# Linear attention with a gated projection on one core: the softmax statistics of q spread in two half transfers, a third batch sent down the same route, and a new order of all steps

## The chip, the core and the metric

One core of a Trainium2 chip runs one program. The core has TensorE (PE, matmuls, with its weight loads shown as PEld), VectorE (DVE), ScalarE (ACT), GpSimd (POOL), SyncE (SP, which here issues every DMA) and 16 DMA engines. The metric is the device time of one execution in microseconds (us); lower is better.

## What is computed

There are 8 batches of 8 heads, 576 positions and 64 channels per head, all float32 (the weights arrive as 64-bit words and are turned into float32 on the chip).

```python
q_s = exp(q - max(q, axis=-1));  q_s = q_s / (sum(q_s, axis=-1) + 1e-9)     # over the 64 channels
k_s = exp(k - max(k, axis=2));   k_s = k_s / (sum(k_s, axis=2) + 1e-9)      # over the 576 positions
kv  = einsum('bhsd,bhse->bhde', k_s, v)
x   = einsum('bhsd,bhde->bhse', q_s, kv)      # then 8 heads side by side: 576 x 512 per batch
gate = sigmoid(sum over 5 taps j of conv_w[j] * x shifted by 4 - j positions)
out  = (gate * (x @ w_val)) @ w_out
```

## The kernel before

The program is a list of about 1,100 short steps, `ORDER`, written out in full; each entry names a function, its indices, the engine (`a` = ACT, `v` = DVE, `p` = POOL) and the buffer slots that it takes (`@n`). Every engine works its own steps strictly in the order of that list, SP its DMAs too, and waits on semaphores wherever a step needs the result or the buffer of another. So the order of the list sets the time.

Per batch `b` the work runs as follows. `load_k`, `k_peak`, `k_row`, `k_spread`, `k_sub` and `k_exp` make the exponentials of k (the column maxima go to DRAM as one row, and a DMA, `k_spread`, brings that row back into all 128 partitions as the tile `kmax`). `kv` multiplies k and v on PE, `kv_norm` scales the result. `attend b g` (L506) makes two of the four x tiles, each in a PSUM bank pair of its own. Each x tile is then read by `x_high` and `x_low` (the value split into two parts for matmuls), `first` and four `tap` steps, which build the gate; a tap with `v` is one DVE instruction (L530), a tap with `a` is a product on ACT (L533) and an addition on POOL (L534). `sigmoid`, `value` (L548, 6 matmuls), `gated` (L553), `g_high`, `g_low`, `project` (L575, 3 matmuls) and `store` finish it.

The softmax of q must end with channels on the partitions, because `attend` contracts over them. There are two routes:

- **By rows and a transpose** (batches 0 to 3): `q_max`, `q_sub`, `q_exp`, `q_sum`, `q_over`, `q_mul` normalise q with positions on the partitions; `q_turn` and `tail_turn` transpose it on PE, and `q_turned` and `tail_turned` copy it out of PSUM on ACT.
- **By rows and channels** (batches 4 to 7): q is loaded a second time with channels on the partitions (`load_qc`, 1152 KB). The row copy gives only statistics: `q_log` makes max + ln(sum), `stat_turn` and `stat_turned` transpose them, `q_row` (L449, L451) writes them to DRAM as two rows of 9,216 bytes, one for each half of the partitions, and `q_spread` (L456) brings them back as a tile `qsp` in which the first row fills partitions 0 to 63 and the second row partitions 64 to 127, 1152 KB. Four `qc_sub` steps (L460, on POOL or DVE) subtract that tile from q, and two `qc_exp` (L464, ACT) finish. `qc_sub` reads all 128 partitions of `qsp`, so it needs both rows' halves.

The spread of a batch is one DMA with the access pattern [2, 64, 2304]: the outermost dimension is the two rows, the second repeats a row 64 times with a step of zero, and the last is the row.

Of the kernel before, what the change touches and what calls it, by code (L numbers as in the profile page):

```python
# [16 lines left out]
B, H, S, D = 8, 8, 576, 64  # L17
# [25 lines left out]
    tail_turned 0 a @5, kv 0 @2, part 3 a @9, load_words 0 @4, field 0 @1, q_mul 0 2 a, part 0 a @0, joined 2,
    w_high 2 a, scaled 0 a, load_kc 1 2 3 @6, q_mul 0 1 p, q_sub 1 4 v, q_mul 0 3 p, q_turn 0 0 @0, load_kc 1 3 4,
    k_top 1 2 @1, k_raise 1 2, q_turned 0 0 a, kv_norm 0 v @0, attend 0 0 @1 @2, k_top 1 3, joined 3, load_kc 1 1 2,
    k_top 1 1, load_words 5 @5, k_raise 1 3, signed 0, field 5 @5, w_low 2 p, warm 0 @1, k_raise 1 1, load_kc 1 0 1,
    k_top 1 0, x_high 0 1 a @6, x_low 0 1, joined 8, first 0 1 a @7, tap 0 1 1 v, tap 0 1 3 v, q_sub 1 3 p,
    tap 0 1 0 v, x_high 0 0 a @0, x_low 0 0, first 0 0 a @4, load_q 5 @7, joined 0, q_turn 0 1 @0, q_turned 0 1 a,
    tap 0 0 1 v, joined 4, tap 0 1 2 a @2, w_high 0 a, q_sub 1 0 p, tap 0 0 2 v, k_raise 1 0, tap 0 0 3 v, w_high 3 a,
    attend 0 1 @0 @2, w_low 3 p, x_high 0 2 a @1, tap 0 0 0 v, warm 11 @0, first 0 2 a @3, tap 0 2 1 v, tap 0 2 3 v,  # L50
    w_high 4 p, w_low 4 p, tap 0 2 0 v, load_words 6 @2, x_low 0 2, tap 0 2 2 a @1, k_tail_turn 1 @1, scaled 5 a,
    warm 6 @0, x_high 0 3 a @3, load_words 7 @4, x_low 0 3, k_turn 1 0 @1, k_turned 1 0 a @1, q_exp 1, part 5 a @6,
# [5 lines left out]
    kv_norm 1 v @1, q_mul 1 3 p, q_mul 1 2 p, q_turn 1 0 @2, scaled 7 a, q_turned 1 0 a, q_turn 1 1 @0,
    q_turned 1 1 a, g_low 0 1 p, load_q 3 @5, load_km 2 0 @7, k_peak 2 0, signed 7, signed 6, load_q 2 @6,
    g_high 0 0 a, load_km 2 1 @4, attend 1 0 @1 @2, load_km 2 3 @8, w_high 5 p, first 1 1 a @1, tap 1 1 0 v,  # L60
    tap 1 1 3 v, w_low 5 p, value 0 2 3 @0, sigmoid 0 2, g_low 0 0 p, value 0 2 0, tap 1 1 2 v, part 7 a @7,
    x_high 1 0 a @5, project 0 0 1 @1, value 0 2 2, x_high 1 1 a @4, x_low 1 1, joined 7, first 1 0 a @6, tap 1 0 0 v,
    part 6 a @5, joined 6, load_v 2 @0, tap 1 1 1 a @0, sigmoid 0 3, k_peak 2 3, tap 1 0 3 v, tap 1 0 2 a @2,
    value 0 2 1, gated 0 2 @8, w_high 6 a, project 0 1 1 @0, w_low 6 p, project 0 0 0, k_peak 2 1, k_row 2, x_low 1 0,
    value 0 3 3 @2, w_high 7 a, value 0 3 1, g_high 0 2 a, g_low 0 2 p, value 0 3 2, q_max 2 @0, tap 1 0 1 a @0,
    value 0 3 0, gated 0 3 @3, attend 1 1 @0 @1, load_k 2 @1, x_high 1 2 a @2, first 1 3 a @4, w_low 7 p, tap 1 3 3 v,
    x_low 1 2, sigmoid 1 1, project 0 1 0, x_high 1 3 a @3, x_low 1 3, g_high 0 3 a, tap 1 3 2 v, load_km 4 0 @2,
    project 0 0 2, first 1 2 a @5, k_spread 2 @8, tap 1 2 2 v, load_km 3 3 @9, project 0 1 2, value 1 2 1 @2,
    k_peak 4 0 @1, value 1 2 0, g_low 0 3 p, value 1 2 2, sigmoid 1 0, tap 1 2 3 v, project 0 0 3, q_sub 2 3 p,
    load_km 3 2 @0, value 1 2 3, store 0 0 a @7, q_sub 2 0 p, project 0 1 3, store 0 1 a @3, project 0 2 0 @1,  # L70
    q_sub 2 2 p, tap 1 2 1 v, tap 1 2 0 v, q_sub 2 4 p, sigmoid 1 2, tap 1 3 0 v, tap 1 3 1 v, project 0 2 1,
    project 0 2 2, project 0 2 3, value 1 3 2 @0, gated 1 2 @2, sigmoid 1 3, k_sub 2 0 v, q_max 3 @1, load_km 4 1 @7,
# [15 lines left out]
    project 0 5 0, load_k 4 @0, q_mul 3 0 p, x_high 2 2 a @3, tap 2 1 1 a @6, tap 2 3 3 v, tap 2 2 0 v, project 0 4 2,
    value 2 2 1 @2, q_mul 3 2 p, q_mul 3 1 a, tap 2 2 1 v, k_spread 4 @0, q_sub 4 1 p, k_exp 3, project 0 4 0,
    q_mul 3 4 p, value 2 2 3, value 2 2 0, k_sub 4 2 p, project 0 4 3, store 0 5 a @4, k_sub 4 0 p, kv 3 @0,  # L90
    q_mul 3 3 a, tap 2 2 2 v, x_low 2 2, value 2 2 2, k_peak 5 1 @0, kv_norm 3 v @1, q_turn 3 0 @1, q_sub 4 4 p,
    sigmoid 2 2, tail_turn 3 @1, tail_turned 3 a @3, q_sub 4 3 p, k_peak 5 3, q_sub 4 2 p, gated 2 2 @6, q_max 5 @1,
# [555 lines left out]
```

## Time and profile before

| what | value |
|---|---|
| median of 3 runs | 403.88 us (403.73 to 403.95) |
| the profiled execution, its own time | 404.08 us |
| its span in the trace | 402.3 us |
| mean granted TensorE clock | 0.868 of full speed |
| DMA traffic | 60.74 MB, 151 GB/s over the span |

The trace is of one execution; start times count from the start of its span. A duration of an instruction is what its engine shows; "idle before" names the event that ended a wait. A row of stretches gives, for each engine, busy time and number of instructions, then the granted TensorE clock as a share of full speed, the mean share of the 16 DMA engines that was busy, and what they moved.

### The profile page before, as it was taken

Reading aid. Unit: us, or ns where it says so; the run is one execution under the profiler, and the core shown is the slowest. Engines: PE = TensorE matmul, PEld = TensorE weight load, DVE = VectorE, ACT = ScalarE, POOL = GpSimd, SP = SyncE. Lnnn points to the kernel's source line nnn. Section 1 sums busy time; section 2 is a strip of 40 time slices with the busy share of each in tenths; the row PEclk is TensorE's granted clock in tenths of the full one; section 3 lists DMA queues with packets and bytes.
Section 4 is the critical chain, followed back from the end, with each engine's and each line's share of the span. In section 5 each row is a group of like instructions: output and inputs, shape, how many; then the busy total and the mean of one; then the engine's idle time right before and its main releaser. Section 6 shows DMA issues by size and latency. Waiting matters only on the chain.

```text
span 402.3 us, 5954 instructions
## 1 busy us (share of the span) xinstructions
PE 299.6 (74%) x2292; PEld 252.9 (63%) x2292; DVE 248.4 (62%) x331; ACT 212.8 (53%) x318; POOL 204.6 (51%) x182
## 2 busy tenths in 40 slices
PE   6565699998969979407950886913977349999998
PEld 6553498787748859306740675912875346989987
DVE  4997698989798877408970377705886034364111
ACT  2885697758779586506720658702725014753110
POOL 3743764898789766008503946006472161856230
PEclk9585889999999998956995696975989959999999
DMA  8997057478765574511621771214601110011022
GB/s 299 416 364 265 28 203 268 101 269 314 171 246 201 149 226 163 173 53 53 204 91 51 261 286 63 100 54 170 222 31 48 76 47 26 28 52 54 26 97 88
DMA packets 17604, 60.74 MB, mean 151 GB/s; under 512 B 2856, under 2 KB 3112, under 8 KB 13864
## 3 DMA queue, kind: packets, MB, share of 16 engines
q1 hardware_dynamic: 17576, 60.36, 42.8%
q8 instruction: 18, 0.29, 0.3%
q14 instruction: 10, 0.08, 0.1%
HBM read 50.83 MB, written 9.52 MB: 150 GB/s over the span
## 4 chain that ended last, share of the span: by engine, by line
DMA 27%; PE 26%; DVE 25%; issue 11%; ACT 7%; POOL 4%; SPq 1%; ACTq 0%; DVEq 0%; POOLq 0%
DMA qsp<-qrow 13%; PE out L575 10%; PE val L548 9%; DVE gate L530 8%; DMA km<-in_k_strided 6%; DMA out<-o 5%; DVE qs L389 3%; DVE kpk L303 2%; DVE g L553 2%; PE x L506 2%; DVE xx L516 2%; PE kv L478 2%; DMA q<-in_q 2%; DVE qm L371 2%; ACT xx L218 1%
## 5 line engine op out<-in xcount | busy, mean ns | idle before, releaser
L530 DVE SCALAR_TENSOR_TENSOR gate<-x,cw,gate 128x575 f32<-128x575 f32 (+3 forms) x94 | 75.2, 810 | 31.7 <-ACT gate L522 25.1
L548 PE MATMUL val<-xx,w_val_hi 128*128 128x288 f32 x512 | 92.4, 304 | 0.0
L548 PEld LDWEIGHTS val<-xx,w_val_hi 128*128 128x128 f32 x512 | 79.1, 198 | 0.0
L548 PE MATMUL val<-xx,w_val_lo 128*128 128x288 f32 x256 | 59.0, 313 | 24.5 <-DVE kvd L490 17.5
L534 POOL TENSOR_TENSOR gate<-gate,far 128x574 f32<-128x574 f32 (+3 forms) x34 | 43.9, 1291 | 45.9 <-ACT far L533 45.5
L548 PEld LDWEIGHTS val<-xx,w_val_lo 128*128 128x128 f32 x256 | 45.6, 199 | 32.8 <-issue 17.7
L575 PE MATMUL out<-w_out_lo,gh 128*128 128x512 f32 x144 | 60.3, 419 | 3.3 <-ACT o L218 3.0
L575 PE MATMUL out<-w_out_hi,gl 128*128 128x512 f32 x144 | 58.3, 405 | 0.0
L575 PE MATMUL out<-w_out_hi,gh 128*128 128x512 f32 x144 | 58.2, 404 | 0.0
L506 PE MATMUL x<-qT,kvd 64*64 64x288 f32 x256 | 25.0, 486 | 40.2 <-ACT far L533 16.8
L460 POOL TENSOR_TENSOR qT<-qT,qsp 128x576 f32<-128x576 f32 x10 | 16.1, 1613 | 71.9 <-DMA qsp<-qrow 71.9
L566 POOL TENSOR_TENSOR gl<-g,gh 128x576 fp32r<-128x576 f32 x27 | 38.2, 1421 | 26.4 <-ACT gh L218 18.2
L506 PEld LDWEIGHTS x<-qT,kvd 64*64 64x64 f32 x256 | 10.5, 152 | 49.6 <-POOL gl L566 16.4
L533 ACT ACTIVATE far<-x,cw 128x574 f32<-128x574 f32 (+3 forms) x34 | 24.7, 740 | 24.1 <-DVE gate L530 14.4
L320 POOL TENSOR_TENSOR k<-k,kmax 128x512 f32<-128x512 f32 (+1 forms) x32 | 36.3, 1150 | 0.8 <-DMA kmax<-krow 0.2
L575 PEld LDWEIGHTS out<-w_out_lo,gh 128*128 128x128 f32 x144 | 27.9, 194 | 12.6 <-issue 6.6
L553 DVE TENSOR_TENSOR g<-val,gate 128x576 f32<-128x576 f32 x32 | 24.0, 751 | 17.7 <-ACT gate L537 9.3
L478 PE MATMUL kv<-v,k 128*64 128x65 f32 x512 | 21.2, 244 | 15.6 <-DVE g L553 11.3
L575 PEld LDWEIGHTS out<-w_out_hi,gl 128*128 128x128 f32 x144 | 28.0, 194 | 7.5 <-POOL gl L566 1.1
L460 DVE TENSOR_TENSOR qT<-qT,qsp 128x576 f32<-128x576 f32 x6 | 4.5, 754 | 45.2 <-DMA qsp<-qrow 45.2
L379 POOL TENSOR_TENSOR q<-q,qm 128x512 f32<-128x512 f32 (+1 forms) x32 | 30.8, 979 | 2.3 <-issue 2.2
L522 ACT ACTIVATE gate<-x,cw 128x576 f32<-128x576 f32 x27 | 20.0, 747 | 20.6 <-DVE xx L220 6.8
(81 smaller groups left out, 503.2 us busy)
## 6 DMA issues: line engine op xcount, KB each, us to landing
v<-in_v SPq DMA_DIRECT2D x8, 1170.0 KB
out<-o SPq DMA_DIRECT2D x36, 256.0 KB
q<-in_q SPq DMA_DIRECT2D x7, 1152.0 KB
km<-in_k_strided SPq DMA_DIRECT2D x24, 288.0 KB
k<-in_k SPq DMA_DIRECT2D x6, 1152.0 KB
qT<-in_q_channels SPq DMA_DIRECT2D x4, 1152.0 KB
qsp<-qrow SPq DMA_DIRECT2D x4, 1152.0 KB
kc<-in_k_channels SPq DMA_DIRECT2D x8, 288.0 KB
```

The lines of the kernel that those rows point to most:

```text
L320: engine(e).tensor_sub(kk[r, a], kk[r, a], top[r, m])
L379: engine(e).tensor_sub(qq, qq, spread(T["qm", b], h0, h1))
L460: engine(e).tensor_sub(t, t, T["qsp", b][:, n * S:n * S + S])
L478: nc.tensor.matmul(acc[h * D:(h + 1) * D, u, i], kk[:, g], vv[:, g], start=(c == 0), stop=False)
L506: nc.tensor.matmul(x[half][o, t0:t1], kvd[b % 2][r, n], T["qT", b][r, n, t0:t1], start=True, stop=True)
L530: nc.vector.scalar_tensor_tensor(out=a, in0=x, scalar=w, in1=a, op0=ALU.mult, op1=ALU.add)
L533: nc.scalar.activation(far, x, AF.Copy, scale=w)
L534: nc.gpsimd.tensor_add(a, a, far)
L548: nc.tensor.matmul(ps[:, cs], w[:, m, ms], z[:, cs], start=(not at and n == 0), stop=(len(at) == 3 and n == 2))
L553: nc.vector.tensor_mul(T["g", b, m], T["val", b, m], T["gate", b, m])
L566: engine(e).tensor_sub(both("gl", m)[:, s], T["g", b, m], T["gh", m][:, s].bitcast(F32))
L575: nc.tensor.matmul(ps, z, w[:, i], start=(not at and j == 0), stop=(len(at) == 3 and j == 2))
```

## The change

Three things are changed together. First, `q_spread` now takes a half: it is called twice for each batch, and each call brings one row into 64 partitions, with the access pattern [64, 2304]. Second, batch 3's q goes by rows and channels as well: its `q_over`, five `q_mul`, two `q_turn`, two `q_turned`, `tail_turn` and `tail_turned` go, and `load_qc`, `q_log`, `stat_turn`, `stat_turned`, `q_row`, two `q_spread`, four `qc_sub` and two `qc_exp` come in. Third, the whole list is put in another order, in which the steps that read one x tile stand more often in runs of one engine: over the 32 x tiles, the reading engine changes 93 times in the list of before and 63 times in the new one. Some steps change engine with it: 105 taps go to DVE and 23 to ACT and POOL (94 and 34 before), 5 stores are copied out by DVE and 31 by ACT (13 and 23 before), 2 of the `q_sub` are on DVE and 38 on POOL (8 and 32 before).

```diff
-    q_max 4 @0, q_sub 3 0 p, load_km 4 3 @3, load_km 5 3 @8, q_sub 3 4 p, q_exp 3, k_peak 4 3, attend 2 0 @1 @2,
...
-    store 0 3 a @6, q_sum 3 @1, q_over 3, attend 2 1 @1 @0, k_sub 3 3 p, x_low 2 1, project 0 5 1 @1, first 2 3 a @1,
...
-    tap 3 3 2 a @5, k_sub 5 1 p, q_spread 4 @4, value 3 0 1 @1, value 3 0 0, q_exp 5, x_low 3 2, project 1 1 1 @1,
...
-    q_log 7 @1, project 2 3 2, x_low 6 1, qc_sub 6 2 p, value 5 2 1 @2, qc_exp 6 1, g_high 5 3 p, g_low 5 3 p,
...
+    k_peak 4 3, k_peak 4 2, q_sub 3 0 p, store 0 1 a @9, load_qc 3 @0, q_sub 3 3 p, project 0 2 0,
...
+    project 0 3 2 @0, q_log 3 @0, g_low 1 3 p, project 0 6 3, project 0 6 0, store 0 6 a @4, load_km 5 2 @9,
+    project 0 3 3, tap 2 1 0 v, project 0 3 0, first 2 2 a @2, stat_turn 3 @1, k_sub 3 4 p, tap 2 1 3 v,
+    stat_turned 3 a @0, k_sub 3 3 p, k_sub 3 2 p, q_row 3, project 0 3 1, tap 2 2 2 v, k_sub 3 0 p, k_sub 3 1 p,
+    project 0 7 0 @1, first 2 3 a @1, tap 2 2 0 v, k_sub 4 1 p, store 0 3 a @8, tap 2 2 3 a @4, tap 2 1 2 v,
+    tap 2 3 0 v, x_high 2 2 a @1, x_low 2 2, tap 2 3 2 v, project 0 7 2, k_peak 5 2, q_sub 4 2 v, tap 2 3 3 v,
+    tap 2 2 1 v, project 0 7 1, project 0 7 3, project 0 5 2 @0, tap 2 3 1 v, project 0 5 1, q_max 5 @1,
+    tap 2 1 1 a @6, project 0 5 0, k_exp 3, q_spread 3 0 @4, k_sub 4 2 p, value 2 2 2 @2, q_sub 4 3 p, q_spread 3 1,
+    qc_sub 3 1 v, value 2 2 3, value 2 2 0, store 0 7 a @8, load_km 5 0 @9, qc_sub 3 0 v, sigmoid 2 0, sigmoid 2 2,
...
-    def q_spread(b):
-        t = T["qsp", b] = big(f"qsp_{b}", [NB * S])
-        row = T["qrow", b].rearrange("h n (o s) -> h o (n s)", o=1)
-        nc.sync.dma_start(out=t, in_=row.broadcast_to([2, D, NB * S]))
+    def q_spread(b, half):
+        if ("qsp", b) not in T:
+            T["qsp", b] = big(f"qsp_{b}", [NB * S])
+        row = T["qrow", b].rearrange("h n (o s) -> h o (n s)", o=1)[half]
+        nc.sync.dma_start(out=T["qsp", b][half * D:half * D + D], in_=row.broadcast_to([D, NB * S]))
```

## Rows read from the trace of the kernel before

**Rows 1.** The page, part 1: busy time (share of the span) and instructions.

```profile
PE 299.6 (74%) x2292; PEld 252.9 (63%) x2292; DVE 248.4 (62%) x331; ACT 212.8 (53%) x318; POOL 204.6 (51%) x182
```

**Rows 2.** The chain that ended last: start, length, what.

```profile
154.56 27.45 DMA qsp<-qrow
...
200.00 21.39 DMA out<-o
```

**Rows 3.** Stretches in which TensorE stands still: stretch, length, engines, clock, DMA.

```profile
166.40:182.00 15.60, 0.00 (x0) 0.00 (x0) 0.00 (x0) 0.00 (x0) 0.00 (x0) 0.63 0.23 75
...
208.00:222.70 14.70, 0.00 (x0) 0.03 (x1) 1.53 (x2) 1.89 (x3) 4.67 (x4) 0.61 0.11 48
...
263.20:277.70 14.50, 0.04 (x4) 0.04 (x4) 3.10 (x7) 1.16 (x1) 3.26 (x2) 0.59 0.23 77
...
316.00:327.20 11.20, 0.00 (x0) 0.00 (x0) 1.46 (x3) 0.00 (x0) 1.41 (x1) 0.70 0.11 46
```

**Rows 4.** SyncE's timeline: first statistics row, and the four spreads.

```profile
151.43 0.81 SPq L449 DMA_DIRECT2D qrow<-st  x1
...
154.56 0.54 SPq L456 DMA_DIRECT2D qsp<-qrow  x1
...
191.51 0.53 SPq L456 DMA_DIRECT2D qsp<-qrow  x1
...
249.16 0.52 SPq L456 DMA_DIRECT2D qsp<-qrow  x1
...
300.69 0.52 SPq L456 DMA_DIRECT2D qsp<-qrow  x1
```

**Rows 5.** Stretches, for DMA: two kmax spreads; a qsp spread alone; plain loads.

```profile
139.60:142.60 3.00, 2.76 (x21) 2.12 (x23) 2.57 (x4) 2.97 (x4) 1.20 (x1) 1.00 0.90 65
289.20:290.60 1.40, 1.40 (x12) 1.35 (x11) 1.40 (x1) 1.38 (x2) 1.40 (x2) 1.00 0.73 190
210.00:220.00 10.00, 0.00 (x0) 0.00 (x0) 0.00 (x0) 0.00 (x0) 1.97 (x2) 0.56 0.13 54
36.00:39.00 3.00, 0.00 (x0) 0.00 (x0) 2.48 (x4) 0.41 (x1) 0.00 (x0) 0.50 1.03 414
```

**Rows 6.** Waits: who for whom, us in total, times, longest.

```profile
POOL qT L460 <- DMA qsp<-qrow: 71.9, 4, 21.0
...
DVE qT L460 <- DMA qsp<-qrow: 45.2, 3, 16.6
...
ACT far L533 <- DVE gate L530: 14.4, 10, 4.3
ACT xx L218 <- DVE gate L530: 11.6, 9, 4.1
...
ACT far L533 <- DVE xx L516: 8.3, 5, 3.2
```

**Rows 7.** Stretches between the standstills, and one before the first.

```profile
64.60:103.90 39.30, 36.82 (x310) 31.59 (x310) 35.12 (x44) 30.01 (x53) 32.55 (x30) 1.00 0.68 214
...
182.00:208.00 26.00, 22.62 (x197) 18.43 (x197) 24.75 (x38) 16.10 (x19) 14.64 (x12) 0.90 0.40 126
222.70:263.20 40.50, 35.37 (x263) 29.57 (x263) 26.44 (x32) 26.45 (x30) 20.24 (x19) 0.85 0.49 178
277.70:316.00 38.30, 33.13 (x189) 27.73 (x189) 25.98 (x32) 17.48 (x22) 18.33 (x16) 0.89 0.32 118
327.20:402.30 75.10, 72.87 (x483) 62.72 (x483) 26.14 (x36) 27.43 (x41) 31.47 (x25) 0.98 0.14 53
```

**Rows 8.** Groups of instructions by line: busy, mean ns, idle before.

```profile
L530 DVE SCALAR_TENSOR_TENSOR gate<-x,cw,gate 128x575 f32<-128x575 f32 (+3 forms) x94 | 75.2, 810 | 31.7 <-ACT gate L522 25.1 <-POOL gate L534 4.1 <-ACT xx L218 1.2
...
L534 POOL TENSOR_TENSOR gate<-gate,far 128x574 f32<-128x574 f32 (+3 forms) x34 | 43.9, 1291 | 45.9 <-ACT far L533 45.5
...
L220 DVE COPY o<-out 128x512 f32<-128x512 f32 x13 | 8.9, 684 | 15.0 <-PE out L575 15.0
...
L379 DVE TENSOR_TENSOR q<-q,qm 128x512 f32<-128x512 f32 (+1 forms) x8 | 7.2, 916 | 0.1
```

More of the change, by code (lines that the diff above doesn't have):

```diff
@@ L43 @@
[L43 to L52, printed above, removed]
@@ L58 @@
[L58 to L67, printed above, removed]
@@ L68 @@
[L68 to L72, printed above, removed]
@@ L88 @@
[L88 to L92, printed above, removed]
@@ L118 @@
-    x_low 4 2, store 1 3 a @2, first 4 2 a @6, tap 4 2 2 v, tap 4 2 0 v, first 4 3 a @8, tap 4 3 1 v,
-    project 1 2 3 @1, k_row 6, qc_sub 5 0 p, project 1 2 0, tap 4 2 3 v, x_high 4 3 a @5, k_spread 6 @7, qc_sub 5 1 p,
-    project 1 2 2, kv 5 @2, kv_norm 5 v @1, project 1 2 1, g_low 3 2 p, qc_sub 5 3 p, x_low 4 3, g_high 3 3 p,
-    g_low 3 3 p, project 1 6 0 @0, load_k 6 @4, tap 4 3 3 v, qc_exp 5 0, tap 4 2 1 a @9, attend 5 0 @1 @2,
-    tap 4 3 2 v, store 1 2 a @4, first 5 0 a @2, tap 5 0 1 v, project 1 4 1 @1, load_qc 7 @3, x_high 5 0 a @4,
@@ new lines @@
+    first 1 1 a @0, g_low 0 1 p, signed 7, part 7 a @4, load_q 2 @0, load_v 3 @2, first 1 0 a @6, g_high 0 0 a,
+    x_high 1 0 a @5, tap 1 1 3 v, value 0 2 0 @2, value 0 2 3, value 0 2 1, tap 1 1 0 v, w_low 5 p, project 0 1 1 @1,
+    project 0 0 1 @0, tap 1 1 2 v, tap 1 0 0 v, sigmoid 0 2, joined 7, g_low 0 0 p, k_row 2, k_spread 2 @8,
+    x_high 1 1 a @4, x_low 1 0, tap 1 1 1 a @5, tap 1 0 3 v, x_low 1 1, value 0 2 2, gated 0 2 @2, tap 1 0 1 a @1,
+    tap 1 0 2 a @9, project 0 1 0, project 0 0 0, g_high 0 2 a, g_low 0 2 p, q_max 2 @0, q_sub 2 1 p, value 0 3 3 @0,
@@ new lines @@
+    k_sub 4 3 p, tap 3 1 1 v, tap 3 1 3 v, qc_sub 3 3 p, qc_sub 3 2 p, load_k 5 @2, x_low 3 1, tap 3 0 0 a @5,
+    g_high 2 1 a, tap 3 1 0 v, value 2 0 3 @0, tap 3 0 3 a @9, x_high 3 0 a @4, load_qc 4 @3, tap 3 0 1 a @3,
+    tap 3 1 2 v, x_low 3 0, value 2 0 1, value 2 0 2, value 2 0 0, project 0 8 3, project 0 4 3, gated 2 0 @5,
+    project 0 4 0, q_sub 5 4 p, project 0 4 2, load_v 5 @4, qc_exp 3 1, attend 3 1 @1 @2, q_sum 4 @1, k_exp 4,
+    store 0 4 a @0, first 3 3 a @9, g_low 2 1 p, project 0 8 0, value 2 3 1 @0, tap 3 3 0 v, tap 3 3 3 v, k_row 5,
@@ new lines @@
+    load_v 4 @0, tap 3 3 2 v, g_high 2 2 a, q_log 4 @0, project 0 8 1, x_high 3 2 a @5, value 2 3 3, store 0 8 a @3,
+    x_low 3 2, value 2 3 2, value 2 3 0, stat_turn 4 @1, stat_turned 4 v @1, q_row 4, gated 2 3 @7, x_high 3 3 a @6,
+    tap 3 3 1 v, g_low 2 2 p, project 1 0 2 @0, q_sub 5 0 p, x_low 3 3, project 1 3 2 @1, q_max 6 @0, value 3 0 1 @0,
+    value 3 0 2, k_spread 5 @0, first 3 2 a @8, load_km 6 3 @1, tap 3 2 1 v, q_sub 5 3 p, tap 3 2 0 v, g_high 2 0 a,
+    tap 3 2 3 v, q_spread 4 0 @7, q_sub 5 1 p, q_exp 5, g_high 2 3 p, project 1 3 1, sigmoid 3 3, value 3 0 0,
@@ new lines @@
+    tap 3 2 2 v, sigmoid 3 2, kv 4 @2, project 1 0 1, sigmoid 3 0, q_spread 4 1, kv_norm 4 a @0, q_sum 5 @1,
+    sigmoid 3 1, value 3 0 3, gated 3 0 @3, g_low 2 3 p, value 3 2 1 @1, project 1 3 3, k_sub 5 1 p, qc_sub 4 0 v,
+    value 3 2 2, g_low 2 0 p, qc_sub 4 1 v, k_sub 5 3 p, load_km 6 1 @7, q_sub 6 3 p, q_sub 6 4 p, q_log 5 @0,
+    k_peak 6 1 @0, g_high 3 0 a, value 3 2 0, load_qc 5 @0, k_peak 6 3, load_k 6 @5, qc_exp 4 0, k_sub 5 0 p,
+    value 3 2 3, gated 3 2 @5, project 1 3 0, qc_sub 4 3 v, load_km 6 2 @6, g_low 3 0 p, store 1 3 a @7,
@@ new lines @@
+    value 3 1 0 @2, project 1 0 3, project 1 0 0, k_peak 7 3 @1, attend 4 0 @0 @1, store 1 0 a @1, g_high 3 2 a,
+    g_low 3 2 p, q_sub 6 2 p, k_sub 5 4 v, x_high 4 0 a @2, stat_turn 5 @1, qc_sub 4 2 p, first 4 1 a @3, k_sub 5 2 p,
+    x_low 4 0, stat_turned 5 a @0, first 4 0 a @8, project 1 2 3 @0, tap 4 1 0 v, q_row 5, tap 4 1 2 v, tap 4 0 2 v,
+    load_km 6 0 @4, project 1 2 2, value 3 1 3, tap 4 0 0 v, tap 4 1 3 a @5, value 3 1 2, x_high 4 1 a @1,
+    tap 4 1 1 a @7, tap 4 0 3 v, x_low 4 1, project 1 1 1 @1, tap 4 0 1 v, project 1 1 2, project 1 2 0, k_peak 6 2,
@@ new lines @@
+    value 3 1 1, q_sub 6 1 p, gated 3 1 @1, q_sub 6 0 p, k_peak 6 0, project 1 1 0, q_spread 5 0 @6, qc_exp 4 1,
+    q_spread 5 1, attend 4 1 @1 @0, x_high 4 3 a @0, project 1 2 1, store 1 2 v @0, first 4 3 a @5, tap 4 3 0 v,
+    x_low 4 3, k_row 6, k_spread 6 @6, value 3 3 2 @2, load_km 7 2 @2, project 1 1 3, tap 4 3 3 v, project 1 6 2 @0,
+    tap 4 3 1 v, project 1 6 0, first 4 2 a @7, tap 4 2 1 a @4, x_high 4 2 a @5, tap 4 3 2 v, qc_sub 5 0 p,
+    tap 4 2 0 v, load_qc 6 @7, value 3 3 3, k_exp 5, q_exp 6, x_low 4 2, qc_sub 5 1 p, value 3 3 1, value 3 3 0,
@@ new lines @@
+    tap 5 0 1 a @9, tap 5 0 2 v, value 4 1 0 @2, stat_turn 6 @0, project 1 5 1, load_v 6 @2, qc_sub 5 2 p,
+    stat_turned 6 a @1, q_row 6, value 4 1 1, project 1 5 0, project 1 4 0 @0, value 4 1 2, store 1 5 a @7,
+    tap 5 0 3 v, qc_sub 5 3 p, x_high 5 1 a @3, x_low 5 1, value 4 1 3, sigmoid 4 1, gated 4 1 @9, project 1 4 1,
+    q_spread 6 1 @4, project 1 4 3, value 4 0 2 @1, value 4 0 0, sigmoid 4 0, qc_exp 5 1, q_max 7 @1, value 4 0 3,
+    value 4 0 1, gated 4 0 @0, attend 5 1 @0 @2, value 4 3 3 @1, q_spread 6 0, sigmoid 4 3, first 5 2 a @7,
@@ new lines @@
+    value 4 3 2, k_sub 6 2 p, sigmoid 5 0, first 5 3 v @3, tap 5 2 1 v, x_high 5 3 a @4, tap 5 3 1 v, k_sub 6 1 p,
+    load_v 7 @1, tap 5 3 2 v, q_sub 7 1 p, q_sub 7 0 p, sigmoid 5 1, tap 5 3 0 v, x_high 5 2 a @0, x_low 5 2,
+    project 1 4 2, project 1 8 0 @1, store 1 4 a @8, value 4 3 0, project 1 8 3, value 4 3 1, tap 5 3 3 v,
+    k_sub 6 0 p, project 1 8 2, x_low 5 3, k_exp 6, tap 5 2 0 v, q_sub 7 3 p, project 1 8 1, store 1 8 a @6,
+    q_sub 7 2 v, qc_sub 6 3 p, qc_sub 6 0 v, tap 5 2 2 v, project 1 7 0 @0, qc_sub 6 1 v, kv 6 @2, qc_sub 6 2 p,
@@ new lines @@
+    project 2 2 3, k_spread 7 @9, project 2 2 0, first 6 0 a @6, tap 6 0 1 v, tap 6 0 2 v, x_low 6 0, tap 6 0 3 v,
+    store 2 2 a @8, k_sub 7 1 p, stat_turn 7 @0, tap 6 0 0 v, stat_turned 7 a @0, load_qc 7 @0, value 5 2 1 @1,
+    q_row 7, q_spread 7 0 @4, k_sub 7 2 p, k_sub 7 3 p, qc_exp 6 1, project 2 0 0 @1, value 5 2 0, value 5 2 3,
+    value 5 2 2, project 2 3 2 @0, gated 5 2 @3, g_high 5 2 p, tap 6 1 1 v, project 2 3 1, attend 6 1 @2 @1,
+    first 6 3 a @0, tap 6 1 2 v, tap 6 3 2 v, tap 6 3 1 v, tap 6 3 3 v, first 6 2 v @8, value 5 1 3 @0, q_spread 7 1,
```

192 lines of the change are left out of this document (89 added, 103 removed).

## The prediction

> **What bounds the kernel now.** Start with the busy line of the page [rows 1]. No engine is busy more than 74% of the span, and TensorE and VectorE, at 299.6 and 248.4 us, leave over 100 us each. So the time is not that of one saturated engine; the question is where the engines stand together. The chain that ended last answers it: its longest piece is 27.45 us of the transfer that spreads batch 4's q statistics, and another, 21.39 us, is a store that was issued behind batch 5's spread [rows 2]. Next I cut the span where TensorE stops [rows 3]. There are four such stretches, of 15.6, 14.7, 14.5 and 11.2 us, 56.0 us together, and TensorE is busy for 0.04 us in all of them. Each follows one of the four spreads, issued 11.8, 16.5, 14.0 and 15.3 us before it [rows 3, 4]. The waits name the same cause: POOL's and DVE's `qc_sub` wait 71.9 and 45.2 us for `qsp` [rows 6].
>
> The DMA column says why a spread is so slow. In a stretch in which nothing but a spread moves, 0.13 of the 16 engines is busy, which is 2 of 16, at 54 GB/s, 27 GB/s for each; plain loads run at a share of 1.0 and 414 GB/s, 26 GB/s for each of 16 [rows 5]. So each engine works at full rate, and 14 have nothing to do. The pattern's outermost dimension is 2.
>
> Between the standstills the work is dense: TensorE is busy 85% or more of each stretch, and VectorE 24.75 of 26.0 us in one [rows 7].
>
> **The spread in halves.** A half has 64 as its outermost dimension. The trace holds no DMA into 64 partitions. The nearest is `k_spread`, which repeats one DRAM row 128 times and shows shares of 0.73 and 0.90, so it uses most or all engines; its rate, though, is 65 GB/s in one case and 190 in the other [rows 5]. Repeating one row can thus be slow even on all engines. For the 1.18 MB of both halves that gives 18 us at 65, 6.2 at 190 and 2.9 at the loads' 414. I take 6: the row here is 9,216 bytes against 2,048, two engines read it at full rate each, and 190 is the middle.
>
> For the number of engines of a half the Trainium skill has a rule ("DMA: Bandwidth & Descriptors", section "Why a DMA increments its semaphore by 16 and not by 1"): the largest number up to 16 that divides the slowest dimension larger than one of both sides, so 2 for the old pattern and 16 for a half. The 0.13 agrees with its 2 [rows 5]; for 64 no row here can tell, and by the rule alone, without the hot row, the spread would be the 2.9 us above.
>
> Is 6 us hidden? In the new list DVE has 12 steps between `q_row 3` and its first `qc_sub 3`, 8 of them taps at 0.81 us and one a maximum over all of q; at 0.81 each they are 9.7 us, with the longer maximum about 11 [rows 8]. From the first statistics row to the spread SP needed 3.1 us [rows 4]. That leaves about 8 us for the transfer; batch 4 has 11 such steps with a maximum and a sum among them, much the same. So a spread of 6 us costs nothing, and the cover is gone from 8 us on: each further us is paid five times. With the spreads hidden all four standstills go: **-56.0 us**. The stores and loads that queue on the two busy engines behind a spread come free too; their wait lies inside the same stretches, so it isn't counted again.
>
> **Batch 3 by rows and channels.** It adds 1152 KB of `load_qc` and 1152 KB of spreads. At 414 GB/s [rows 5] that is 2.9 us of all DMA engines each, in a part of the span where the DMA share is at most 0.68 [rows 7], so it is hidden if SP issues it early enough; `load_qc 3` stands about 80 steps before its first use. SP gets 6 more spreads and 3 more statistics rows, some 5 us of issuing at 0.5 to 0.8 us each [rows 4]. Behind a waiting spread stand the loads of later batches. The transposes that go spare TensorE about 2 us and ACT its multiplications; neither is the engine that ends the stretches there, so I count nothing for them.
>
> **Steps that change engine.** On DVE, 11 more taps are 8.9 us; 8 fewer stores are -5.5 and 6 fewer `q_sub` -5.5 [rows 8]. The rest, one to three steps of a kind, most of them additions (three `first`, three `qc_sub`, two additions for `q_log`), I bound between 0 and +7 at some 0.8 us a step. Together -2 to +5; DVE is close to the limit between the standstills, so I price it in full: **+2 us**. POOL loses 11 additions of 1.29 us and takes the `q_sub`; it is busy 51% of the span and ACT 53%, so their change is covered by their idle time [rows 1, 8].
>
> **Readers by engine.** ACT waits 14.4, 11.6 and 8.3 us for DVE steps that read or build from the same x tile [rows 6], 34.3 us in 24 waits. Changes of reader fall from 93 to 63; a third of 34.3 is 11 us. ACT isn't the bound, so the gain for the end lies between 0 and 11; nearer to the lower end, since ACT has slack: **-4 us**.
>
> **The clock.** Within the standstills the granted clock is 0.59 to 0.70 [rows 3], and after them it stays low: 0.90, 0.85, 0.89 and 0.98 over the following stretches, against 1.00 from 64.6 to 103.9 us, where TensorE never stops for long [rows 7]. The low level is 1.2 GHz of 2.4. Time lost to it, if TensorE set the pace throughout, is (1 - clock) x length: 2.6 + 6.1 + 4.2 + 1.5 = 14.4 us. With the standstills gone it comes back in part; VectorE binds as well, so between 0 and 14: **-7 us**.
>
> **The sum.** The profiled execution took 404.08 us: 404.1 - 56.0 + 2 - 4 - 7 = 339.1. The median of the runs is 0.2 us below that execution, so **339 us**. With all bounds of this case, 404.1 - 56 - 2 - 11 - 14 = 321 and 404.1 - 56 + 5 = 353.
>
> **Rivals.**
> *The halves use all engines, but one repeated row is slow.* For it speaks the 65 GB/s at a share of 0.90 [rows 5]; against it the 190 and the full 27 GB/s of each of two engines. At 65 GB/s a spread lasts 18 us, 10 beyond the cover, five times: 339 + 50 = 389. At 98 GB/s it lasts 12: 339 + 20 = 359. I take 355 to 389 as its span.
>
> *The halves are no quicker than the whole: slower than before.* If the two halves follow one another at the pace of the one transfer, the spread again lasts the 25 us and more that it now takes from issue to its first reader (27.45 for batch 4 [rows 2]), at the same place, ahead of `qc_sub`, but in five batches instead of four: 26 - 8 = 18 us, five times 18 is 90, and 339 + 90 = 429. The point from which this decides is a spread of (404 - 339) / 5 + 8 = 21 us. Against it speaks the idle share of 14 engines [rows 5], which a dimension of 64 can fill. The Trainium skill has a rule for this side ("DMA: Bandwidth & Descriptors", section "Rules for kernel authors"): two transfers to disjoint halves of the partitions aren't worth it, because both use the same engines and serialize. It presupposes that the single transfer fills all 16; here the row shows 2, so I give it little.
>
> *The order packs better than the sum says.* With no standstill, the time falls below 321 if TensorE and VectorE overlap better than the 85 to 95% that TensorE reaches now [rows 7]. Nothing in the trace speaks for it but the fewer changes of reader.
>
> **How the numbers follow.** Forecast (321 to 353): 0.75. Slow repeated row (355 to 389): 0.15. Halves as slow as the whole (429): 0.05. Better packing (below 321): 0.05. The range 322 to 368 leaves out the last two and most of the slow row's span above its first third, and holds about 0.8. A change of 0.2% is about what a measurement of this kernel can tell from none; faster by more has 0.94, slower by more 0.05, the same 0.01.
>
> **What would show it.** Right: while a spread is under way the DMA share is near 1, not 0.13; `qc_sub`'s waits for `qsp` fall from 117 us to under 15; no stretch over 5 us without TensorE after the first 60 us; a mean granted clock above 0.92; ACT's waits for DVE's tap and `x_low` steps below 25 us. Wrong: `qsp` still among the longest pieces of the chain; spreads over 8 us from issue to first reader, with TensorE idle behind them, now with batch 3's among them; or a TensorE that waits for DVE where it waited for DMA, with DVE's busy time well above 254 us.

## The result, and the profile after

The changed kernel takes 313.81 us (median of 4 runs, 313.27 to 315.65); the kernel before, on the same chip, 403.91 (403.73 to 406.45). The ratio is 0.7766 [0.7721, 0.7811]: 90 us less. The forecast was 339 us, in a range of 322 to 368: the sign is right, and the gain is larger than the range allowed. The profiled execution took 315.65 us, 313.9 of them its span, at a mean granted clock of 0.962 (before: 0.868).

First the page of the changed kernel: busy time (as in [rows 1]), then the span in 40 slices of 7.8 us (busy tenths of TensorE and of VectorE, the granted clock, the DMA share).

```profile
PE 283.5 (90%) x2275; PEld 237.6 (76%) x2275; DVE 246.9 (79%) x334; ACT 202.8 (65%) x292; POOL 194.5 (62%) x173
...
PE   8176779989998898989978999999999999999998
...
DVE  3999899999979999999599989899896964422300
...
PEclk9876579999999999999999999999999999999999
DMA  7997794936498579948977396963552100100222
```

From the eighth slice on (55 us) TensorE is busy 80% or more of every slice but one, a 7 that stands beside an 8 and a 9. A stop of over 5 us would take as much from one slice or two neighbouring ones; no two of these lack more than 2.4 + 1.6. So the four standstills of [rows 3] are gone, and the clock does not fall again. TensorE is idle for 313.9 - 283.5 = 30.4 us, where it was 402.3 - 299.6 = 102.7 [rows 1, 3].

The spreads, as issued by SyncE (timeline; start, length of issuing, instruction), now five times two:

```profile
111.46 1.15 SPq L457 DMA_DIRECT2D qsp<-qrow  x2
145.34 1.14 SPq L457 DMA_DIRECT2D qsp<-qrow  x2
...
229.91 1.14 SPq L457 DMA_DIRECT2D qsp<-qrow  x2
```

While each of the five is under way (windows; columns as in [rows 3], with the clock, DMA share and GB/s last):

```profile
112.30:118.80 6.50, 6.50 (x44) 5.92 (x43) 6.50 (x8) 6.44 (x7) 5.60 (x5) 1.00 0.91 214
146.00:153.00 7.00, 7.00 (x108) 6.30 (x107) 6.86 (x9) 5.71 (x11) 4.39 (x4) 1.00 1.03 224
167.00:174.00 7.00, 5.77 (x39) 3.92 (x38) 6.67 (x11) 4.94 (x9) 4.63 (x4) 1.00 0.77 188
196.00:203.00 7.00, 7.00 (x57) 6.04 (x56) 5.66 (x6) 6.83 (x9) 6.67 (x7) 1.00 0.91 206
230.50:237.50 7.00, 7.00 (x45) 6.36 (x43) 6.31 (x9) 2.89 (x3) 4.61 (x4) 1.00 0.75 185
```

The DMA share is 0.75 to 1.03 and not 0.13, the rate 185 to 224 GB/s and not 54 [rows 5], and TensorE works through it, in four of the five without a break. In the first four stretches other transfers run beside the spread; in the last SyncE issues nothing else until 236.34 us, so 0.75 and 185 GB/s are nearly the spread's own. In the chain that ended last the second half of a spread is now a piece of 7.5 us (27.45 for the whole before [rows 2]):

```profile
112.02 7.56 DMA qsp<-qrow
...
145.89 7.50 DMA qsp<-qrow
153.40 3.44 issue
156.84 0.55 DVE qT L461
```

From the issue of its first half to the first `qc_sub` that reads it, a spread takes 8.0 to 11.5 us; the longest is batch 4's (145.34 to 156.84).

And the waits (who waits for whom: us in total, times, longest), beside [rows 6]:

```profile
ACT far L534 <- DVE gate L531: 10.8, 6, 2.5
...
ACT xx L218 <- DVE gate L531: 4.0, 3, 1.6
...
POOL qT L461 <- DMA qsp<-qrow: 3.1, 3, 2.5
...
DVE qT L461 <- DMA qsp<-qrow: 1.4, 2, 1.1
```

The waits that the profile puts down to `qsp` fell from 117.1 us to 4.5. To these belong, most likely, the 3.44 us before batch 4's `qc_sub` in the chain above, for which it names no cause. The waits between ACT and DVE on an x tile fell as well, and by more than the prediction thought of; the experiments return to that.

### The profile page after: what moved, and what is told of

Its sections match the earlier page's. It is cut to its first block, busy times and chain, and to the rows that moved or that the text cites. A ratio compares the mean times of both kernels' runs of the same rounds, so it can differ in the third digit from the quotient of the medians.

```text
span 313.9 us, 5888 instructions
## 1 busy us (share of the span) xinstructions
PE 283.5 (90%) x2275; PEld 237.6 (76%) x2275; DVE 246.9 (79%) x334; ACT 202.8 (65%) x292; POOL 194.5 (62%) x173
## 4 chain that ended last, share of the span: by engine, by line
PE 45%; DVE 30%; DMA 9%; issue 7%; ACT 5%; POOL 1%; SPq 1%; DVEq 0%; ACTq 0%; POOLq 0%
PE out L576 20%; PE val L549 18%; DVE gate L531 9%; DMA qsp<-qrow 5%; PE x L507 4%; DVE xx L517 3%; DVE qs L389 3%; DVE kpk L303 3%; DVE g L554 2%; DMA km<-in_k_strided 2%; DVE e L285 2%; DMA words<-in_w_val 2%; DVE k L320 1%; PE kv L479 1%; ACT gate L523 1%
## 5 line engine op out<-in xcount | busy, mean ns | idle before, releaser
L531 DVE SCALAR_TENSOR_TENSOR gate<-x,cw,gate 128x575 f32<-128x575 f32 (+3 forms) x105 | 84.0, 810 | 11.3 <-POOL gate L535 6.6
L549 PE MATMUL val<-xx,w_val_hi 128*128 128x288 f32 x512 | 88.6, 295 | 0.0
L549 PEld LDWEIGHTS val<-xx,w_val_hi 128*128 128x128 f32 x512 | 75.0, 188 | 0.0
L549 PEld LDWEIGHTS val<-xx,w_val_lo 128*128 128x128 f32 x256 | 42.7, 188 | 9.9 <-DVE g L554 2.9
L320 POOL TENSOR_TENSOR k<-k,kmax 128x512 f32<-128x512 f32 (+1 forms) x32 | 37.6, 1188 | 13.4 <-DMA kmax<-krow 13.0
L535 POOL TENSOR_TENSOR gate<-gate,far 128x573 f32<-128x573 f32 (+3 forms) x23 | 29.6, 1290 | 25.6 <-ACT far L534 20.2
L379 POOL TENSOR_TENSOR q<-q,qm 128x512 f32<-128x512 f32 (+1 forms) x38 | 36.5, 984 | 2.3 <-DVE qm L371 1.9
L218 ACT COPY o<-out 128x512 f32<-128x512 f32 x31 | 18.0, 584 | 27.3 <-PE out L576 27.3
L576 PEld LDWEIGHTS out<-w_out_hi,gh 128*128 128x128 f32 x144 | 27.1, 188 | 3.4
L534 ACT ACTIVATE far<-x,cw 128x573 f32<-128x573 f32 (+3 forms) x23 | 16.9, 745 | 15.5 <-DVE gate L531 10.8
L538 ACT ACTIVATE gate<-gate 128x576 f32<-128x576 f32 x32 | 21.1, 682 | 6.8 <-DVE gate L531 4.9
L523 ACT ACTIVATE gate<-x,cw 128x576 f32<-128x576 f32 x24 | 17.7, 744 | 11.3 <-issue 4.5
```

Of the source, the lines that this page charges most:

```text
L218: nc.scalar.copy(out=out, in_=in_)
L320: engine(e).tensor_sub(kk[r, a], kk[r, a], top[r, m])
L379: engine(e).tensor_sub(qq, qq, spread(T["qm", b], h0, h1))
L523: nc.scalar.activation(a, x, AF.Copy, scale=w)
L531: nc.vector.scalar_tensor_tensor(out=a, in0=x, scalar=w, in1=a, op0=ALU.mult, op1=ALU.add)
L535: nc.gpsimd.tensor_add(a, a, far)
```

## The experiments

Times are medians, beside runs of the kernel before on the same chip (about 404 us each time). "Old list" is the order of the kernel before, "new list" that of the changed one. A *change of reader* is counted as in the section on the change: 93 in the old list, 63 in the new. In the code cuts steps of the list stand one to a line, and `...` stands for what is left out.

### What the halves are worth

**The old list with the spread in halves**, nothing else changed:

```
-q_spread 4 @4,
+q_spread 4 0 @4, q_spread 4 1,        # likewise batches 5, 6, 7
```

> The list of before, with only the spread taken in two halves. Theory 1 (a slow spread costs its standstill and the cold clock behind it, nothing else; what the sum missed is the new order's): 404 - 56 - 7 = 341 us, between 335 and 347. Theory 2 (the slow spread also held loads and stores on its two DMA engines, so part of the idle time between the standstills was its doing): 318 to 328 us.

Measured: 344.21 us (341.98 to 346.43), ratio 0.8477 [0.8419, 0.8534], clock 0.941. The halves alone bring 60 us, as the first theory expected: TensorE's idle time falls by 50.9 us against the kernel before (102.7 to 51.8), its busy time, at a higher clock, by 6.7 (299.6 to 292.9). `qsp` is out of the chain. From the trace of this kernel, waits and then two stretches, from the first `attend` of batch 6 to that of batch 7 and from there to the end:

```profile
PE sps L442 <- DVE stat L438: 10.2, 4, 4.3
...
DVE gate L533 <- ACT gate L525: 9.7, 10, 1.7
...
DVE xx L519 <- ACT xx L220: 7.5, 7, 2.4
```

```profile
232.50:275.60 43.10, 37.00 (x283) 31.26 (x282) 31.62 (x41) 19.10 (x24) 21.67 (x17) 0.92 0.33 104
275.60:344.70 69.10, 66.88 (x395) 57.52 (x394) 23.32 (x30) 25.68 (x39) 26.80 (x21) 1.00 0.14 54
```

Cut at the first `attend` of batches 0, 2, 4, 6 and 7, the stretches are 72.6, 68.3, 60.7, 43.1 and 69.1 us long here, and 62.9, 66.5, 53.9, 28.7 and 71.8 in the changed kernel. So what the new list adds to the halves is won before batch 7, and not evenly: 9.7 us in batches 0 and 1, 1.8 in 2 and 3, 6.8 in 4 and 5, and 14.4 in batch 6, the stretch shown, with TensorE idle for 6 us and a clock of 0.92. Over the whole span TensorE idles for 344.7 - 292.9 = 51.8 us here and 30.4 in the changed kernel: 21.4 of the 30.8 us between the two spans is idle time of TensorE, and 9.4 is shorter busy time (clock 0.941 to 0.962, and 17 matrix instructions fewer).

**The new list with the whole spread:**

```
 def q_spread(b, half):
+    if ("qsp", b) in T:
+        return
...
-    nc.sync.dma_start(out=T["qsp", b][half * D:half * D + D], in_=row.broadcast_to([D, NB * S]))
+    nc.sync.dma_start(out=t, in_=row.broadcast_to([2, D, NB * S]))
```

> The changed kernel, with the spread of a batch again as one transfer with the outermost dimension 2. Theory 1: five spreads of about 26 us in place of about 8, with about 8 us of cover: 5 x 18 = 90 us more, 404 us, between 395 and 415, so the new order alone gains nothing. Theory 2 (loads and stores held up too): over 415 us. If the new order were dense by itself and hid the spreads, under 350 us.

Measured: 413.52 us (412.33 to 414.89), ratio 1.0207 [1.0151, 1.0262], clock 0.855. The waits of this kernel:

```profile
DVE qT L462 <- DMA qsp<-qrow: 79.3, 4, 24.9
POOL qT L462 <- DMA qsp<-qrow: 75.4, 4, 20.4
```

With the old transfer the new list is 2% slower than the kernel before: 99.7 us lie between this kernel and the changed one, 20 for each of five spreads, where the four standstills of before were 56.0 us [rows 3]. That is the mechanism of the prediction's slower rival, at about the price it gave (18 beyond the cover of each spread), in a kernel in which its condition holds.

### What limits a half

**Distinct rows.** Each half reads 64 different rows of q instead of one row 64 times:

```
-row = T["qrow", b].rearrange("h n (o s) -> h o (n s)", o=1)[half]
-nc.sync.dma_start(out=..., in_=row.broadcast_to([D, NB * S]))
+rows = qc[b, half * D:half * D + D].rearrange("p n s -> p (n s)")
+nc.sync.dma_start(out=..., in_=rows)
```

> The changed kernel, but each half of the spread reads 64 different rows of the q channels from DRAM in place of one repeated row, same bytes and same engines; the values subtracted are then not the statistics, and the transfer doesn't wait for them. If the repeated row is what holds the spread to about 190 GB/s, the transfer runs at 350 to 414 GB/s and lands in 4 to 5 us; if it is the 64 partitions or the half size, it stays near 190. The time falls by 0 to 3 us, since the waits for the spread are 4.6 us in all.

Measured: 313.37 us (311.55 to 313.55), ratio 0.7738 [0.7709, 0.7766]. Three of the stretches with a spread under way:

```profile
110.20:116.70 6.50, 6.50 (x43) 5.88 (x42) 6.50 (x9) 6.44 (x7) 6.38 (x5) 1.00 0.94 220
...
164.00:170.00 6.00, 6.00 (x41) 4.48 (x41) 5.67 (x9) 3.95 (x7) 4.64 (x4) 1.00 1.04 246
...
221.20:227.00 5.80, 5.80 (x46) 4.54 (x45) 4.69 (x7) 0.74 (x1) 5.66 (x7) 1.00 1.02 288
```

220 to 288 GB/s over the five (in the last with batch 7's `load_qc`, issued at 217.97 us, beside it), and 7.6 us to landing for the one half whose landing the profile gives, as in the changed kernel. So the repeated row isn't the main reason why a half runs at about half the rate of the plain loads (414 GB/s [rows 5]); the 350 to 414 GB/s that it would have held back did not come.

**Halves by columns.** The same rows, but each transfer brings half of the columns into all 128 partitions:

```
+w = NB * S // 2
+rows = qc[b].rearrange("p n s -> p (n s)")[:, half * w:half * w + w]
+nc.sync.dma_start(out=T["qsp", b][:, half * w:half * w + w], in_=rows)
```

> As the kernel with distinct rows, which moved at 220 to 250 GB/s where the repeated row moved at 185 to 224, but each half is all 128 partitions by half of the columns, again 576 KB. If the 64 partitions of a half limit the transfer, it now runs at 350 to 414 GB/s; if it is the size of 576 KB or what runs beside it, it stays at 220 to 250. Time 309 to 314 us in both cases. The values subtracted are not the statistics.

Measured: 310.19 us (309.75 to 312.17), ratio 0.7686 [0.7659, 0.7714]. DMA issues of this kernel (KB each, median us from issue to landing), and two stretches with a spread under way:

```profile
qsp<-in_q_channels SPq DMA_DIRECT2D x10, 576.0 KB, 5.0
```

```profile
163.00:167.00 4.00, 4.00 (x27) 3.06 (x29) 3.93 (x6) 2.86 (x4) 3.21 (x3) 1.00 0.93 340
...
220.50:224.50 4.00, 4.00 (x35) 3.08 (x35) 2.90 (x5) 0.74 (x1) 3.93 (x5) 1.00 0.98 330
```

The same bytes land in 5.0 us and not 7.6 (again one half each), at 246 to 340 GB/s over the five, for much the same share of engine time; with the same `load_km` beside batch 5's spread it is 340 against 246 GB/s. That is faster than with 64 partitions and short of the 350 to 414 expected. What differs is that the rows go to 128 partitions instead of 64 and are half as long. The whole kernel gains little from it, about 3 us over the distinct rows: most of the transfer was hidden already.

### Readers by engine, in the new list

**Mixed again.** 17 of DVE's steps on x tiles are moved so that they stand between ACT's on the same tile: 93 changes of reader, as in the old list. Engines, tiles and transfers stay.

```
 first 0 1 a @5,
+tap 0 1 2 v,
 x_high 0 1 a @6,
...
-tap 0 1 2 v,
```

> The changed kernel with 17 DVE readers of x tiles moved forward by at most 15 steps to stand between two ACT readers, so that the reading engine changes 93 times and not 63, as in the list of before. Theory R1: 8 to 20 us slower, 322 to 334 us. Theory R2: 313 to 317 us.

Measured: 335.46 us (334.83 to 337.1), ratio 0.8285 [0.8238, 0.8332]: 21.6 us more than the changed kernel. `x_high` (`xx` on ACT) and `tap` (`gate` on DVE) both only read the x tile and write different tiles; all the same they never run at once: at each of the 93 changes the second reader starts 0.03 us or more after the first has ended. The waits of this kernel:

```profile
ACT xx L219 <- DVE gate L532: 15.7, 10, 3.3
...
ACT far L535 <- DVE gate L532: 13.8, 7, 3.0
DVE gate L532 <- ACT gate L524: 10.1, 8, 4.3
```

**Control.** 17 steps moved as far, so that the 63 changes stay:

```
 w_high 0 a,
+x_low 0 1,
 w_high 4 a,
...
-x_low 0 1,
```

> Control for the readers mixed in the new order (335.5 us): 17 DVE readers of x tiles moved forward by the same distances, 108 steps in all, but none past another reader of its tile, so that the reading engine still changes 63 times. If it is the changes of reader that cost the 21 us (theory R1): 313 to 318 us. If any disturbance of the list costs it (theory S, the order is only dense as it stands): 328 to 340 us.

Measured: 317.37 us (315.25 to 317.96), ratio 0.7852 [0.7826, 0.7877]. **A second control**, with other DVE steps on x tiles:

```
 q_turned 0 1 a,
+x_low 0 0,
 x_low 0 1,
...
-x_low 0 0,
```

> A second control for the mixed readers: 17 other DVE readers, drawn by chance over all x tiles, moved forward by the same distances, none past another reader of its tile (63 changes). Theory R1 (it is the changes of reader that cost): 313 to 320 us, like the first control (317.4). Theory S (the first control fell on harmless places): 325 us or more.

Measured: 315.82 us (314.18 to 317.18), ratio 0.7819 [0.7779, 0.7859]. The controls lie 3.6 and 2.0 us above the changed kernel, the second within the noise; the other 18 to 20 of the 21.6 belong to the changes of reader.

**Half of the moves** (9 of the 17, 75 changes):

```
 tap 0 0 1 a @6,
+tap 0 0 3 v,
 x_high 0 0 a @0,
...
```

> Every other one of the 17 moves that mixed the readers in the new order: the reading engine changes 75 times (63 in the new list, 93 with all moves, which cost 18 us over the control). If each change costs about the same (theory R1, 0.6 us a change): 321 to 325 us. If a few places make the cost: 314 to 319 or 328 to 336 us.

Measured: 323.11 us (321.82 to 323.27), ratio 0.7998 [0.7972, 0.8024]: 9.3 us for 12 changes, 21.6 for 30, or 0.8 and 0.7 us for each. These are means: cut at the first `attend` of each batch, the stretches of batches 0 and 4 hold 4.5 and 7.7 of the 19.2 us by which the mixed kernel's span is longer, and that of batch 0 holds 4.4 of the half mixed one's 6.1. **Three more groupings** than the changed kernel has (57 changes):

```
-x_low 0 3,
 scaled 5 a,
...
 first 0 3 a @3,
+x_low 0 3,
```

> The changed kernel with three more places grouped (x_low of two tiles and one tap moved behind an ACT reader): 57 changes in place of 63. At 0.6 us a change it would be 3 to 4 us below 313.8; if what is left is no longer on the path, 313 to 316 us.

Measured: 314.84 us (313.91 to 316.85), ratio 0.78 [0.7771, 0.7829]: no gain.

In each trace I add up the lines of the waits view in which ACT waits for DVE, or DVE for ACT, and both instructions are on tiles `gate`, `far` or `xx` (the steps on an x tile; a `sigmoid` that waits for its last tap counts too, 2.5 us in the old list and 4.9 in each of the others):

| kernel | changes | ACT for DVE, us | DVE for ACT, us | time, us |
|---|---|---|---|---|
| old list, halves | 93 | 47.0 | 18.4 | 344.2 |
| changed kernel | 63 | 21.5 | 3.3 | 313.8 |
| control | 63 | 20.9 | 6.8 | 317.4 |
| second control | 63 | 19.4 | 5.1 | 315.8 |
| half mixed | 75 | 29.4 | 8.9 | 323.1 |
| mixed | 93 | 44.3 | 14.3 | 335.5 |

From the changed kernel to the mixed one these waits grow by 33.8 us and the time by 21.6 (0.64 of it); to the half mixed one by 13.5 and 9.3 (0.69). So the time grows here by about two thirds of what these waits grow.

### Batch 3's route

**Batch 3 transposed in the new list**, as in the old one: `load_qc 3`, `q_row 3`, `q_spread 3` and what belongs to them go, and five `q_mul`, two `q_turn`, two `q_turned` and the tail's pair come in at nearby places that I chose.

```
-load_qc 3 @0,
...
-stat_turned 3 a @0,
+q_mul 3 0 p, q_mul 3 1 a,
...
-q_spread 3 0 @4,
```

> The changed kernel with batch 3's q by the transposes again: q_over, five q_mul (three on POOL, two on ACT), two q_turn, two q_turned, tail_turn and tail_turned stand where the statistics steps and qc steps of batch 3 stood; everything else keeps its place. Theory P (the 30 us between the old order with halves, 344, and the new, 314, are the order's; the route of one batch is worth what its rows say, a few us of ACT and PE): 313 to 319 us. Theory Q (the route of batch 3 is a main part of the 30): 325 us or more.

Measured: 327.18 us (326.76 to 330.16), ratio 0.8105 [0.8065, 0.8145]: 13.4 us more. The waits of this kernel, first SyncE's between 120 and 150 us, then PE's over the span:

```profile
SPq L236 <- PE qps L409: 16.5, 1, 16.5
...
PE kv L479 <- DMA v<-in_v: 7.1, 1, 7.1
```

L236 is `load_q 6`, which takes the buffer of batch 3's q; L409 is `q_turn`, which reads it last. By rows and channels that buffer is free once the statistics are made, and SyncE issues `load_q 6` at 120.55 us; here it stands for 16.5 us and issues it at 140.50. Four loads stand behind it in the same queue, among them `load_v 4`, issued at 145.01 and not 137.57. All five loads now move at once, this one takes 15.7 us to land, and PE's `kv 4` waits 7.1 us for it. `attend 3 0`, too, starts 6.3 us later (131.2 and not 124.9); PE and ACT make the transposed q just before it, but that this is the reason was not tried by itself. The stretches of batches 2 and 3 are 79.7 us long here and 66.5 in the changed kernel, nearly the whole loss; in the old list with halves, which has the same route, they are 68.3. So the 13.4 us are the price of these transposes at these places in the new list, not what the old list paid for the route.

**Both undone**, batch 3 and the 17 moves:

```
-load_qc 3 @0,                          # and all of "batch 3 transposed"
+tap 0 1 2 v,                           # and all of "mixed again"
```

> The changed kernel with batch 3's q by the transposes (alone 327.2) and the readers mixed by the same 17 moves (alone 335.5). Theory A (the two add up and are together what the new list has over the old with halves): 327.2 + 335.5 - 313.8 = 349, between 344 and 354, as high as the old list with halves (344.2). Theory B (they cost the same idle time twice, the rest of the 30 us is the packing of the list): 335 to 341 us.

Measured: 351.5 us (350.13 to 352.77), ratio 0.8702 [0.8654, 0.8749]. 13.4 + 21.6 = 35.0 would give 348.8; it is 37.7. The two prices about add up, and with both undone the new list is no better than the old one with halves (344.2). But the time is not lost where it was won. From the first `attend` of batch 5 to that of batch 7, in the old list with halves, the changed kernel and this one:

```profile
192.70:275.60 82.90, 70.42 (x545) 59.70 (x545) 61.49 (x80) 46.69 (x55) 45.44 (x38) 0.92 0.49 163
182.90:242.10 59.20, 58.03 (x500) 48.23 (x499) 52.04 (x73) 40.32 (x50) 39.83 (x35) 1.00 0.63 205
215.60:275.10 59.50, 57.80 (x500) 48.39 (x499) 52.37 (x73) 38.02 (x47) 35.13 (x31) 1.00 0.58 179
```

Here the new list is 23.7 us shorter. 11.3 of them are idle time of TensorE, over half of the 21.4 that it saves in all; the rest is a higher clock, and 45 matrix instructions that stand elsewhere in the list. With both parts undone it keeps all but 0.3 of the 23.7. What the two parts cost lies in batches 0 to 4, which take 161.8 us in the old list with halves, 152.8 in the changed kernel and 185.2 here.

### The same repairs in the old list

All three start from the old list with halves (344.2 us). **Readers grouped** (at 19 places, 93 to 56 changes):

```
 x_high 0 1 a @6,
-x_low 0 1,
 joined 8,
 first 0 1 a @7,
+x_low 0 1,
```

> The list of before with halves, and 19 places where one or two DVE readers of an x tile stood between two ACT readers: they are moved behind the ACT reader, by at most 15 steps, so that the reading engine changes 56 times and not 93. Theory R1 (changes of the reader are what kept the old order loose): 10 to 25 us below the kernel with halves alone. Theory R2 (an engine that waits for a reader would have waited for something else): within 3 us of it.

Measured: 348.26 us (347.45 to 349.87), ratio 0.86 [0.8552, 0.8648]. No gain, rather 4 us more, which neither theory expected, though the waits of the table above fall from 65.4 to 51.1 us. **The new engines** (11 taps from ACT to DVE, 8 stores from DVE to ACT, 6 `q_sub` from DVE to POOL):

```
-tap 2 0 3 a @3,
+tap 2 0 3 v,
```

> The list of before with halves, and the engine of steps changed to the numbers of the new list: 11 taps of batches 2, 6 and 7 from ACT and POOL to DVE, 8 stores from DVE to ACT, 6 q_sub from DVE to POOL; the order stays. Theory E (the old list was loose because ACT taps hand the gate from DVE to ACT to POOL and back, 49 us of POOL waiting): 8 to 20 us below 344. Theory P (the gain lies in the order itself): 338 to 348 us.

Measured: 342.69 to 351.2 us; the ratio of the two shorter of its four runs is 0.8523 [0.8457, 0.8588], or 344.7 us: no gain that this spread can show. (Its changes of reader fall to 81 with the engines.) **Statistics later** in batches 4, 6 and 7, because of the wait for `stat` shown under the halves:

```
-stat_turn 4 @1, stat_turned 4 v @0,
...
+stat_turn 4 @1, stat_turned 4 v @0,
+q_row 4,
 q_spread 4 0 @4,
```

> The list of before with halves, and the transpose of the statistics of batches 4, 6 and 7 moved 3 to 5 TensorE steps back in the list (with the steps that hang on it), because TensorE stood 10.2 us in front of it in four waits. Theory W (each such wait lengthens the end): 335 to 339 us. Theory N (TensorE finds another wait in its place, the old list is loose everywhere): 341 to 347 us.

Measured: 350.06 us (348.09 to 352.49), ratio 0.8667 [0.8627, 0.8706]: 6 us worse, beyond both theories. Later statistics cost more behind them than PE's wait for `stat` did.

## Why the prediction was right in sign and short in size

**The bound and the halves (-56.0): right.** Two DMA engines of 16 moved the spread and everything stood behind it; with 64 as the outermost dimension the share went to 0.75 to 1.03. The Trainium skill's rule that the prediction weighed ("DMA: Bandwidth & Descriptors", section "Why a DMA increments its semaphore by 16 and not by 1") agrees with that; its rule against two transfers to disjoint halves (section "Rules for kernel authors") does not hold for this pattern, by the 60 us. For the rate of 190 GB/s that I took, the stretches show 185 to 224, with what moves beside a spread. A spread takes longer than the 6 us: 7.5 us for a half, 8.0 to 11.5 from first issue to first reader, at the edge of the cover of 8 us or beyond it. Some 8 us of waits are left (4.5 that the profile names and batch 4's 3.44).

**The clock (-7, between 0 and 14): right.** From the eighth slice on it is 0.9 or more. In the old list with halves, with the same 2292 matrix instructions, TensorE's busy time is 6.7 us shorter at a clock of 0.941 (0.868 before).

**Steps that change engine (+2): near nothing.** DVE's busy time is 246.9 us against 248.4 [rows 1], 1.5 us less; the new engines alone, in the old list, move nothing that the interval can tell.

**What the new list adds (+2 - 4 + 0 = -2, by its bounds -13 to +5): the step that failed.** From the old list with halves to the changed kernel it is -30 us (344.2 to 313.8). The sum let TensorE's idle time outside the four standstills stay nearly as it was; it is 102.7 - 56.0 = 46.7 us before, 51.8 in the old list with halves and 30.4 in the changed kernel. Two of its terms were tried by undoing them.

**Readers by engine (-4, between -11 and 0): too small.** The term reads: "a third of 34.3 is 11 us. ACT isn't the bound, so the gain for the end lies between 0 and 11". In the new list 30 changes are worth 18 to 20 us. It was wrong in three ways. I took ACT's waits for DVE alone, and three lines of them; all such waits, in both directions, fell from 65.4 us (old list, halves) to 24.8. I scaled by the count of changes; the three lines themselves fell from 34.3 us to 14.8, by 19.5. And I let ACT's idle share of 47% absorb most of it; in the new list the time grows by two thirds of what the waits grow. My reading, only argued, is that in a dense list ACT's next step is what DVE, POOL or PE waits for next; an average idle share does not say that a given wait is free.

**Batch 3's route (0): wrong in the new list.** "neither is the engine that ends the stretches there, so I count nothing for them" looked at busy time and at DMA share. What the route changes is how long batch 3's q holds its buffer, and with it SyncE's queue: 13.4 us when undone. Part of that figure, perhaps most, is due to the places that I gave the transposes: in the old list, with the transposes, the same stretches are only 1.8 us longer than in the changed kernel.

**The sum.** 404 - 60 (halves and clock; the prediction's terms for them are 63) leaves 344, and the new list takes 30 off that. Readers by engine and batch 3's route, 18 and 13, have the size of these 30, but that is in part chance: over half of the idle time that TensorE is spared lies in batches 5 and 6, and stays spared with both undone. What spares it was not found; no run undid that part of the list.

**The rivals.** *One repeated row is slow*: refuted as the main reason, as a half of distinct rows lands in the same 7.6 us; the loss of rate is there, and shrinks when a half fills 128 partitions with rows half as long. *Halves as slow as the whole*: refuted by the shares, and its price confirmed with the whole transfer (413.5 us). *The order packs better than the sum says*, with a chance of 0.05: this is what happened. I wrote that nothing spoke for it but the changes of reader. They are part of it; the rest, batches 5 and 6 above all, is open.

**The signs of being right** all came as written: share near 1, `qsp` waits of 4.5 us, or 8 (under 15), no long stop of TensorE after 60 us, clock 0.962 (over 0.92), ACT's waits for tap and `x_low` steps 21.5 us in all (under 25), DVE's busy time under 254. They bore out the direction, and none could have shown that the sum was too small. Of the signs of being wrong one came in small: batch 4's spread took 11.5 us to its first reader, and TensorE stood 1.97 us before the `attend` behind it.

**What stays open.** What makes batches 5 and 6 so much denser in the new list. And why the old list gains nothing from grouped readers, where the new one loses 18 us without them. There the waits for the other engine shrink and the time doesn't; some other limit must take over, and neither the engines nor the place of the statistics proved to be it. Batch 3's route was not tried in the old list. So "readers 18, batch 3 13" are prices in the new list, each with the other present, and not gains to be had by adding either to the old one.

## What to carry to other kernels

Where a transfer is slow, read the DMA share beside its rate: 0.13 with a full rate per engine meant here that the pattern, with an outermost dimension of 2, gave work to 2 engines of 16, and cutting it in two so that the dimension becomes 64 was worth 60 of 404 us. When an order written by hand changes as a whole, price each wait between engines in both directions and follow each buffer to the load that takes it next: here one load stood for 16.5 us, with four behind it, because a step read its buffer later. To learn what a part of an order is worth, undo it in the new order, with a control that moves as many steps as far; added to the old order it can show nothing. Then compare where the time is lost with where the change had won it: two parts can have the size of the gain and lie elsewhere.
